# Last head group of the numerator in four matmuls of 108 rows, and the output projection held behind the numerator

## The chip, the cores and the metric

The kernel runs on one core of one Trainium2 chip. The metric is device time of one execution in microseconds (us), the median of three runs. The engines are PE (TensorE), DVE (VectorE), ACT (ScalarE), POOL (GpSimd) and SP (SyncE, which here only issues DMAs).

## The reference

A layer of linear attention with a learned feature map, beside a gated feed-forward network, for 2048 rows of width 576, 32 heads of 18 columns, and a hidden width of 4608 (fp32, cut to what matters):

```python
xn = layernorm(x)
qkv = xn @ wqkv                                   # 576 -> 3 x 576
pq, pk = q @ w_phi, k @ w_phi                     # per head, 18 x 18
phi_q = concat(softmax(pq), softmax(-pq))         # 36 features per head
phi_k = concat(softmax(pk), softmax(-pk))
kv = einsum("bhsf,bhsd->bhfd", phi_k, v)          # 36 x 18 per head
num = einsum("bhqf,bhfd->bhqd", phi_q, kv)        # the numerator
den = einsum("bhqf,bhf->bhq", phi_q, phi_k.sum(s)) + 1e-6
s = (num / den) @ wo                              # 576 x 576
ffn = (silu(xn @ w_gate) * (xn @ w_up)) @ w_down  # 576 -> 4608 -> 576
return x + s * silu(ffn)
```

## The kernel before

Most fp32 operands are split into a rounded fp32r part and a rest (`split`, L61: an ACT cast to `hi` and a DVE subtraction to `lo`), and a product is then three matmuls: hi by hi, hi by lo, lo by hi.

The program has these stages. Layer norm and the k and v side end in `kvp`, the sums of phi_k by v, one block for each head group and each sign of the softmax. A head group is seven heads, 126 columns; the fifth and last group has only four, 72 columns (`GROUPS`, `NL` = 72). The blocks are masked to the heads' own diagonal and split into `KVH` and `KVL` (L556 to L560).

The Q stage (loop over n near the end of the listing) goes over 2048 rows in eight passes of 256. `q_tile` computes phi_q times 1/den for 128 rows into the tile `e` (two signs by 576 columns): matmuls into the PSUM tile `p2`, of which there is one, then a chain on DVE and ACT (maximum, subtraction L316, exp, sums, `ez` L616, reciprocal, product L626). `numer` takes the two tiles of a pass and does for each head group four transposes (L638), a split of the 256 x 2 result into `ph` and `pl`, and six matmuls of 256 columns (L645: three products for each of two signs). The result goes, split again, into `oh` and `ol`; the last group's goes into `om` (named km), 108 rows deep: its hi part on 72 rows, and half of its lo part on 36 rows that two small DMAs from `lo` fill (L653). `project` multiplies by wo (L672, 14 matmuls of 288 columns for each of four half tiles), and ACT copies the result out (L678).

In the loop, `numer` of a pass comes first, then the two `q_tile`s of the next, then `project`. A list scheduler puts the instructions of each engine in order; the first four units of the feed-forward network's gate and up products (`early_tile`, matmuls into `pe`, L96) have low priority, and the scheduler puts their matmuls where PE would else wait. Those left over when the last `project` is issued run behind it. Their result goes to DRAM (`h_dram`, L136).

Then comes the main stage: for each further unit SP loads raw weights (`ld`, L738), POOL forms sums and differences of weight blocks (`ts`, L766 to L769), ACT and DVE split them into `w`, SP stores them (`w_dram`) and loads the small tails `wt`. The products px, py and pw (L790, L828) and the down product `pd` (L911) follow. The memory of `ld` is that of the Q stage, so the first load waits for the last wo matmul. This stage is not touched by the change.

## Time and profile before

| | before |
|---|---|
| median of 3 runs | 1592.99 us (1592.48 to 1593.02) |
| the profiled execution | 1592.74 us, of which the span is 1590.6 |
| PE busy | 1578.2 us, 99% of the span, 9383 matmuls |
| DVE, ACT, POOL busy | 1166.5, 724.8, 662.3 us |
| granted clock of TensorE | 0.999 of full speed, mean of the span |
| first matmul behind the last wo matmul | 457.65 us |
| first matmul of the main stage | 475.81 us |

Times in the trace count from the start of the span. Busy time on PE overlaps, since matmuls are pipelined: a row's duration is longer than the distance to the next row's start, and it is the distance that costs time.

### The profile page before, as it was taken

How to read it: one execution, taken by the hardware profiler on the slowest of the kernel's cores; microseconds unless marked ns; L12 is line 12 of the kernel's file. 1: busy time of each engine (PE TensorE's matmuls, PEld its weight loads, DVE VectorE, ACT ScalarE, POOL GpSimd, SP SyncE). 2: the span in 40 equal slices, each digit the busy share in tenths (PEclk: the TensorE clock that was granted, in tenths of full speed). 3: DMA queues.
4: the chain of work that ended last, by engine and by line, in shares of the span. 5: the costliest groups of instructions: out<-in, count | busy, mean ns of one | idle time of the engine just before them, and what ended most of it. 6: DMA issues, size and time to landing. Idle time of an engine off the chain costs nothing.

```text
span 1590.6 us, 25333 instructions
## 1 busy us (share of the span) xinstructions
PE 1578.2 (99%) x9383; PEld 1416.1 (89%) x9383; DVE 1166.5 (73%) x1729; ACT 724.8 (46%) x1403; POOL 662.3 (42%) x714
## 2 busy tenths in 40 slices
PE   9999999999999999999999999999999999999998
PEld 6899998999988988988888898888888888888887
DVE  7777769999946778887777778645767667666677
ACT  5633345455435654454544554454443343333334
POOL 3676762433116535554545445223324324133133
PEclk9999999999999999999999999999999999999999
DMA  9622244445447554555455453974545655555445
GB/s 306 200 82 81 95 145 129 119 122 163 165 175 245 174 178 174 176 177 180 174 174 200 163 186 116 337 219 151 154 139 156 192 177 160 176 184 184 142 118 179
DMA packets 124044, 269.03 MB, mean 169 GB/s; under 512 B 13194, under 2 KB 54858, under 8 KB 122642
## 3 DMA queue, kind: packets, MB, share of 16 engines
q1 hardware_dynamic: 108476, 245.49, 47.2%
q0 software_dynamic: 3552, 12.59, 2.7%
q10 hardware_dynamic: 11894, 9.35, 1.8%
q8 instruction: 74, 1.21, 0.3%
q14 instruction: 48, 0.39, 0.1%
HBM read 167.53 MB, written 99.09 MB: 168 GB/s over the span
## 4 chain that ended last, share of the span: by engine, by line
PE 67%; DVE 1%; POOL 1%; DMA 0%; issue 0%; ACT 0%; SPq 0%; POOLq 0%
PE px L790 25%; PE pd L911 24%; PE pw L790 12%; PE py L790 6%; DMA hb<-h_dram 0%; POOL acc L949 0%; PE pe L96 0%; DVE w L63 0%; DVE hh L63 0%; DMA out<-acc 0%; ACT w L62 0%; POOL ld L769 0%; DVE X L940 0%; POOL ha L1050 0%; DVE X L1073 0%
## 5 line engine op out<-in xcount | busy, mean ns | idle before, releaser
L911 PEld LDWEIGHTS pd<-dw,hh 128*128 128x128 f32 x3012 | 423.4, 188 | 22.4 <-ACT pd L966 1.5
L911 PE MATMUL pd<-dw,hh 128*128 128x288 f32 x3012 | 437.6, 295 | 1.9 <-ACT pd L966 0.7
L790 PE MATMUL px<-X,w 128*128 128x512 f32 x1512 | 385.7, 390 | 0.0
L790 PEld LDWEIGHTS px<-X,w 128*128 128x128 f32 x1512 | 274.6, 188 | 46.0
L790 PE MATMUL pw<-X,w 128*128 128x512 f32 x744 | 188.8, 389 | 0.0
L790 PEld LDWEIGHTS pw<-X,w 128*128 128x128 f32 x744 | 139.6, 188 | 28.9
L1073 DVE TENSOR_TENSOR acc<-pd,acc 128x576 f32<-128x576 f32 x128 | 96.2, 752 | 92.7 <-PE pd L911 92.1
L824 DVE TENSOR_TENSOR s<-pw,s 128x512 f32<-128x512 f32 x126 | 86.4, 687 | 90.3 <-ACT s L819 80.0
L819 ACT COPY s<-px 128x512 f32<-128x512 f32 x126 | 73.8, 586 | 145.4 <-PE px L790 145.3
L63 DVE TENSOR_TENSOR hh<-ha,hh 128x512 fp32r<-128x512 f32 x140 | 112.0, 826 | 19.6 <-ACT hh L62 19.3
L62 ACT CAST hh<-ha 128x512 fp32r<-128x512 f32 x140 | 82.7, 619 | 94.2 <-PE pd L911 68.7
L1045 POOL TENSOR_TENSOR hb<-hb 128x512 f32<-128x512 f32 x34 | 46.3, 1362 | 157.5 <-DVE hb L836 156.5
L96 PE MATMUL pe<-X,wh 128*128 128x512 f32 x340 | 106.0, 396 | 1.3 <-DVE h L135 0.6
L63 DVE TENSOR_TENSOR w<-ld,w 128x512 fp32r<-128x512 f32 (+1 forms) x96 | 77.2, 806 | 35.1 <-ACT w L62 34.1
L790 PE MATMUL px<-X,wt 128*128 128x512 f32 x252 | 98.0, 389 | 0.0
L790 PE MATMUL py<-X,w 128*128 128x512 f32 x378 | 96.5, 390 | 0.0
L1058 POOL TENSOR_TENSOR ha<-ha 128x512 f32<-128x512 f32 x34 | 52.6, 1563 | 102.1 <-DVE hh L63 102.1
L766 POOL TENSOR_TENSOR ts<-ld 128x256 f32<-128x256 f32 x32 | 26.8, 837 | 151.3 <-issue 72.6
L1032 POOL TENSOR_TENSOR h<-ha,hb 128x512 f32<-128x512 f32 x34 | 44.3, 1304 | 106.9 <-DVE ha L840 76.3
L62 ACT CAST w<-ld 128x512 fp32r<-128x512 f32 (+1 forms) x96 | 52.7, 550 | 74.9 <-POOL ld L769 42.3
L844 ACT COPY py<-px 128x512 f32<-128x512 f32 x63 | 36.1, 572 | 108.8 <-PE px L790 97.3
L790 PEld LDWEIGHTS py<-X,w 128*128 128x128 f32 x378 | 68.3, 188 | 10.8
(293 smaller groups left out, 3219.7 us busy)
## 6 DMA issues: line engine op xcount, KB each, us to landing
w_dram<-w SPq DMA_DIRECT2D x90, 512.0 KB
w<-w_dram SPq DMA_DIRECT2D x90, 512.0 KB
wt<-t_dram SPq DMA_DIRECT2D x62, 336.0 KB
ld<-in_B_w_gu SPq DMA_DIRECT2D x32, 512.0 KB
rt<-in_B_w_down SPq DMA_DIRECT2D x33, 288.0 KB
rb<-in_B_w_down SPq DMA_DIRECT2D x33, 288.0 KB
w_dram<-w SPq DMA_DIRECT2D x30, 256.0 KB
w<-w_dram SPq DMA_DIRECT2D x30, 256.0 KB
```

The source lines that it names most:

```text
L62: nc.scalar.copy(hi, src)
L63: nc.vector.tensor_sub(lo, src, hi)
L96: last = nc.tensor.matmul(ps, l, r, start=n == 0, stop=n == len(pairs) - 1)
L790: nc.tensor.matmul(ps, l, r, start=first and n == 0, stop=last and n == len(mm) - 1, skip_group_check=True)
L819: snaps.append(nc.scalar.copy(t, ps))
L824: nc.vector.tensor_add(t, ps, t)
L844: copies.append(nc.scalar.copy(yp, xp))
L911: nc.tensor.matmul(ps, l, r, start=first and n == 0 and m == 0, stop=n == len(hs) - 1 and m == 2, skip_group_check=True)
L1032: sub(s, g["h"][0][0], g["h"][0][1])
L1045: nc.gpsimd.tensor_add(a21, a21, g["h"][1][1])
L1058: sub(a12, a12, g["h"][0][0])
L1073: nc.vector.tensor_add(a2, pd[:, :, 0:HALF], a2)
```

## The change

The last head group's two signs are arranged so that 108 rows hold them. ACT makes a second copy of that part of `e` (`et`, two blocks of 108 columns for each sign's 72: the first 54 columns of both signs, then the last 18 columns of both signs three times over). Four transposes of `et` replace four of `e`. The first block gives 108 rows for three matmuls (hi by hi, hi by lo, lo by hi); the second block holds the last 18 columns three times, as hi, hi and lo, so that one matmul does all three products. `KVP`, which holds the matching rows of the masked blocks, is filled once by ten small DMAs from SBUF to SBUF on SP; what they read lies in an old buffer (`phi`). The split of the transposes is one ACT cast of 108 x 512 and two DVE subtractions (108 x 256, 36 x 256). The last group now comes second instead of first in a pass, and the wo matmuls of a pass, the last one excepted, are issued only after `done`, the last numerator matmul of that pass.

```diff
@@ KV blocks
+            km2 = kk.tile([P, 2 * D], F32R, name="phi", bufs=2)[0:NL, 0:4 * NL].rearrange("p (a s n) -> p a s n", a=2, s=2)
+            km2 = [km2[:, a] for a in range(2)]
...
-                split(KVH[0:w, 4 * i:4 * i + n, 0:w], KVL[0:w, 4 * i:4 * i + n, 0:w], km[0:w, 0:n, 0:w])
+                kh, kl = (t[0:w, 4 * i:4 * i + n, 0:w] for t in (KVH, KVL)) if n == 4 else km2
+                split(kh, kl, km[0:w, 0:n, 0:w])
+            KVP = qc.tile([NK, 3, NL], F32R, name="KVP")
+            for s in range(2):
+                for a, t in enumerate(km2):
+                    nc.sync.dma_start(KVP[s * N3:(s + 1) * N3, a].bitcast(F32), t[0:N3, s].bitcast(F32))
+                for b, t in enumerate((km2[0], *km2)):
+                    r = (2 * b + s) * DH
+                    nc.sync.dma_start(KVP[r:r + DH, 2].bitcast(F32), t[N3:NL, s].bitcast(F32))
@@ q_tile
-                return e
+                et = qk.tile([P, 2, NK], F32, name="et", bufs=2)
+                o = GROUPS[-1][0]
+                e2 = e.rearrange("p (s n) -> p s n", s=2)
+                nc.scalar.copy(et[:, 0].rearrange("p (s n) -> p s n", s=2), e2[:, :, o:o + N3])
+                nc.scalar.copy(et[:, 1].rearrange("p (b s n) -> p b s n", b=3, s=2),
+                               e2[:, :, o + N3:D].unsqueeze(1).to_broadcast([P, 3, 2, DH]))
+                return e, et
@@ numer
-                for g in (NG - 1, *range(NG - 1)):
+                for g in (0, NG - 1, *range(1, NG - 1)):
...
+                            src = e[0][:, s * D + o:s * D + o + w] if g < NG - 1 else e[1][:, s]
+                            nc.tensor.transpose(pt[0:w if g < NG - 1 else NK, s, j * P:(j + 1) * P], src, ident)
...
+                    else:
+                        nc.scalar.copy(ph[0:NK], pt[0:NK])
+                        nc.vector.tensor_sub(pl[0:NK, 0], pt[0:NK, 0], ph[0:NK, 0])
+                        nc.vector.tensor_sub(ph[0:2 * DH, 1], pt[0:2 * DH, 1], ph[0:2 * DH, 1])
+                        mm = [(KVP[:, a], p) for a, p in ((0, ph[0:NK, 0]), (1, ph[0:NK, 0]), (0, pl[0:NK, 0]), (2, ph[0:NK, 1]))]
+                    for k, (a, p) in enumerate(mm):
+                        done = nc.tensor.matmul(po[0:w], a, p, start=k == 0, stop=k == len(mm) - 1)
@@ project
-                        for k, (a, bw) in enumerate(mm):
-                            nc.tensor.matmul(ps[:, 0:HALF], a, bw, start=k == 0, stop=k == len(mm) - 1)
+                        with ExitStack() if last else tc.issue_after(done.ins):
+                            for k, (a, bw) in enumerate(mm):
+                                nc.tensor.matmul(ps[:, 0:HALF], a, bw, start=k == 0, stop=k == len(mm) - 1)
```

Line numbers of the changed kernel are higher: L96 becomes L97, L638 becomes L656, L645 becomes L669, L672 becomes L697, L766 to L769 become L791 to L794.

The scheduler's order changes with it. On PE, in the middle of the Q stage, the end of one pass's numerator stood before among the wo matmuls of the same pass (pt is the numerator, p the projection):

```order
L672 MATMUL p<-WOH,ol 128x288
L672 MATMUL p<-WOH,oh 128x288
L672 MATMUL p<-WOL,oh 128x288
L672 MATMUL p<-WOH,ol 128x288
L672 MATMUL p<-WOH,oh 128x288
L645 MATMUL pt<-ph,KVH 126x256 x2
L645 MATMUL pt<-ph,KVL 126x256 x2
L645 MATMUL pt<-pl,KVH 126x256 x2
L672 MATMUL p<-WOL,oh 128x288
L672 MATMUL p<-WOH,ol 128x288
```

In the changed kernel the same place has early matmuls (pe) ahead of the numerator's last six, and the wo matmuls all behind them:

```order
L97 MATMUL pe<-X_61,wh 128x512 x2
L97 MATMUL pe<-X_62,wh 128x512
L97 MATMUL pe<-X_62,wl 128x512
L97 MATMUL pe<-X_62,wh 128x512
L669 MATMUL pt<-ph,KVH 126x256 x2
L669 MATMUL pt<-ph,KVL 126x256 x2
L669 MATMUL pt<-pl,KVH 126x256 x2
L697 MATMUL p<-WOH,oh 128x288
L697 MATMUL p<-WOL,oh 128x288
```

So each pass now has its 56 wo matmuls in one piece, and early matmuls fill what they filled. Over the Q stage, from the first Q matmul to the last wo matmul, 324 early matmuls stand on PE instead of 290; behind the last wo matmul, ahead of the first py, 40 are left instead of 74.

On PE in the first pass, a run of early matmuls stands between the second and the third q tile. These are its last rows before and the first of the third tile (p with the input tile X_64):

```order
L96 MATMUL pe<-X_60,wl 128x512
L96 MATMUL pe<-X_60,wh 128x512 x2
L96 MATMUL pe<-X_61,wh 128x512
L96 MATMUL pe<-X_61,wl 128x512
L96 MATMUL pe<-X_61,wh 128x512 x2
L96 MATMUL pe<-X_61,wl 128x512
L96 MATMUL pe<-X_61,wh 128x512
L96 MATMUL p_2678<-QH,X_64 128x288
```

In the changed kernel the run ends seven matmuls earlier:

```order
L97 MATMUL pe<-X_60,wl 128x512
L97 MATMUL pe<-X_60,wh 128x512
L97 MATMUL p_2695<-QH,X_64 128x288
L97 MATMUL p_2695<-QL,X_64 128x288
L97 MATMUL p_2695<-QH,X_64 128x288 x2
```

It has 19 early matmuls instead of 26; the seven stand further behind, among the 324.

On POOL, at the opening of the main stage, the DMA that stores an early result stood before behind two units' sums:

```order
L603 DMA t_dram<-tl 32x896 x4
L766 TENSOR_TENSOR ts<-ld 128x256
L767 TENSOR_TENSOR ts<-ld,ts 128x256
L768 TENSOR_TENSOR ld<-ld 128x256
L769 TENSOR_TENSOR ld<-ld,ts 128x256
```

In the changed kernel one of these DMAs stands between the first and the second of them:

```order
L614 DMA t_dram<-tl 32x896 x4
L791 TENSOR_TENSOR ts<-ld 128x256
L137 DMA h_dram<-h 128x512
L792 TENSOR_TENSOR ts<-ld,ts 128x256
L793 TENSOR_TENSOR ld<-ld 128x256
L794 TENSOR_TENSOR ld<-ld,ts 128x256
```

The work of POOL, ACT and DVE on the first weights is otherwise in the order of before. The first px matmul writes a PSUM bank that the last early gate tile held; the ACT instruction that empties it (silu, L131) stands on ACT behind all casts of the first weight unit, the last of which waits for L794.

## Rows read from the trace of the kernel before

**Rows 1.** Windows: length; PE, PEld, DVE, ACT, POOL busy; clock; DMA.
```profile
320.00:340.00 20.00, 19.91 (x138) 18.64 (x137) 19.37 (x29) 9.57 (x15) 7.53 (x17) 1.00 0.43 132
...
440.00:460.00 20.00, 19.99 (x131) 17.46 (x130) 7.60 (x13) 7.75 (x16) 0.00 (x0) 1.00 0.13 41
```

**Rows 2.** Timeline of PE, a numerator's first groups: start, duration, line, tiles, count.
```profile
282.14 0.85 PE L638 MATMUL pt<-ident,e 128*72 128x128 f32 x6
282.74 0.48 PE L96 MATMUL pe<-X,wl 128*128 128x512 f32 x1
...
284.66 0.40 PE L645 MATMUL pt<-ph,KVH 72*72 72x256 f32 x2
...
285.37 0.40 PE L645 MATMUL pt<-ph,KVH 126*126 126x256 f32 x2
...
286.08 0.86 PE L96 MATMUL pe<-X,wh 128*128 128x512 f32 x3
```

**Rows 3.** Timeline of PE, eight transposes of 126 columns and what follows.
```profile
263.39 1.04 PE L638 MATMUL pt<-ident,e 128*126 128x128 f32 x8
264.19 0.38 PE L96 MATMUL p<-QL,X 128*128 128x288 f32 x1
```

**Rows 4.** Groups by line and form, weight loads of the transposes: busy, mean ns.
```profile
L638 PEld LDWEIGHTS pt<-ident,e 128*126 128x126 f32 x128 | 14.9, 140 | 1.1 <-issue 0.2 <-DVE lo L651 0.2
...
L638 PEld LDWEIGHTS pt<-ident,e 128*72 128x72 f32 x32 | 3.4, 114 | 1.7 <-DVE e L626 0.9 <-issue 0.3
```

**Rows 5.** Groups by line and form on DVE, 240 to 440 us.
```profile
L63 DVE TENSOR_TENSOR pl<-pt,ph 72x512 fp32r<-72x512 f32 x7 | 4.8, 683 | 0.1
...
L651 DVE TENSOR_TENSOR lo<-pt,km 72x256 fp32r<-72x256 f32 x7 | 2.9, 415 | 0.0
```

**Rows 6.** Timeline of PE, first matmul of the third q tile.
```profile
241.46 0.37 PE L96 MATMUL p<-QH,X 128*128 128x288 f32 x1
```

**Rows 7.** DVE timeline: last KV split, first ez, release of second tile's p2.
```profile
224.81 0.32 DVE L63 TENSOR_TENSOR KVL<-km,KVH 72x144 fp32r<-72x144 f32 x1 [0.38 <-ACT KVH L62]
...
235.80 1.35 DVE L616 TENSOR_TENSOR ez<-e,zb 128x1152 f32<-128x1152 f32 x1
...
240.55 0.76 DVE L316 TENSOR_TENSOR e<-p,m 128x576 f32<-128x576 f32 x1
```

**Rows 8.** Timeline of SP: two small SBUF to SBUF DMAs, first raw weight loads.
```profile
443.73 1.53 SPq L653 DMA_DIRECT2D km<-lo  x2
...
457.89 1.30 SPq L738 DMA_DIRECT2D ld<-in_B_w_gu  x2
```

**Rows 9.** PE timeline: last early matmuls, first of the main stage.
```profile
457.65 0.39 PE L96 MATMUL pe<-X,wh 128*128 128x512 f32 x1
...
464.45 1.21 PE L96 MATMUL pe<-X,wh 128*128 128x512 f32 x3
...
472.46 0.50 PE L96 MATMUL pe<-X,wh 128*128 128x512 f32 x1 [0.63 <-DVE h L135]
...
475.81 0.39 PE L828 MATMUL py<-X,w 128*128 128x512 f32 x1
```

**Rows 10.** Timeline of POOL: the first weight unit's sums.
```profile
463.17 0.73 POOL L766 TENSOR_TENSOR ts<-ld 128x256 f32<-128x256 f32 x1 [50.78 <-DMA ld<-in_B_w_gu]
463.98 1.07 POOL L767 TENSOR_TENSOR ts<-ld,ts 128x256 f32<-128x256 f32 x1
...
465.70 0.74 POOL L769 TENSOR_TENSOR ld<-ld,ts 128x256 f32<-128x256 f32 x1
...
472.86 0.57 POOL L136 DMA_DIRECT2D h_dram<-h  x1 [1.95 <-DVE h L135]
```

**Rows 11.** Timeline of ACT: last cast of the first weight unit, the last silu.
```profile
467.31 0.40 ACT L62 CAST w<-ld 128x256 fp32r<-128x256 f32 x1
...
471.86 0.60 ACT L131 ACTIVATE h<-pe 128x512 f32<-128x512 f32 x1 [0.52 <-PE pe L96]
```

**Rows 12.** Timeline of DVE: an early product at the opening of the main stage.
```profile
464.37 0.68 DVE L135 TENSOR_TENSOR h<-pe,h 128x512 f32<-128x512 f32 x1
```

More of the change, by code (lines that the diff above doesn't have):

```diff
@@ L31 @@
 NK = NL + NL // 2
+N3 = NK // 2
 QS = 256
@@ L531, in gated_hedgehog_kernel @@
             qc = att.enter_context(tc.tile_pool(name="qc", bufs=1, reuse_waits="tile"))
-            KVH = qc.tile([GW, 2 * NG, GW], F32R, name="KVH")
-            KVL = qc.tile([GW, 2 * NG, GW], F32R, name="KVL")
+            KVH = qc.tile([GW, 2 * NG - 2, GW], F32R, name="KVH")
+            KVL = qc.tile([GW, 2 * NG - 2, GW], F32R, name="KVL")
             zb = qc.tile([P, 2 * D], F32, name="zb")
@@ L637, in numer @@
                         for j, e in enumerate(es):
-                            nc.tensor.transpose(pt[0:w, s, j * P:(j + 1) * P], e[:, s * D + o:s * D + o + w], ident)
+                            src = e[0][:, s * D + o:s * D + o + w] if g < NG - 1 else e[1][:, s]
+                            nc.tensor.transpose(pt[0:w if g < NG - 1 else NK, s, j * P:(j + 1) * P], src, ident)
                     ph = qk.tile([GW, 2, QS], F32R, name="ph", bufs=2)
                     pl = qk.tile([GW, 2, QS], F32R, name="pl", bufs=2)
-                    split(ph[0:w], pl[0:w], pt[0:w])
                     po = pt[:, 0]
-                    for k, (a, p) in enumerate(((KVH, ph), (KVL, ph), (KVH, pl))):
-                        for s in range(2):
-                            nc.tensor.matmul(po[0:w], a[0:w, 2 * g + s, 0:w], p[0:w, s], start=k + s == 0, stop=k + s == 3)
+                    if g < NG - 1:
+                        split(ph[0:w], pl[0:w], pt[0:w])
+                        mm = [(a[0:w, 2 * g + s, 0:w], p[0:w, s]) for a, p in ((KVH, ph), (KVL, ph), (KVH, pl)) for s in range(2)]
+                    else:
[5 more added lines that the diff above has]
+                        done = nc.tensor.matmul(po[0:w], a, p, start=k == 0, stop=k == len(mm) - 1)
                     if g < NG - 1:
@@ L653, in numer, with project @@
                         nc.sync.dma_start(om[NL:NK, a].bitcast(F32), lo[a * (NK - NL):a * (NK - NL) + NK - NL].bitcast(F32))
-                return oh, ol, om
-            def project(b, oh, ol, om, last):
+                return oh, ol, om, done
+            def project(b, oh, ol, om, done, last):
                 for j in range(QS // P):
```

## The prediction

> **What bounds the kernel now.** I read the windows first, to see which engine the Q stage waits for. PE is busy for 19.91 of 20 us in the middle of it, while DVE is close behind with 19.37, and ACT has half its time free [rows 1]. Both PE and DVE are nearly full because the scheduler fills PE's waits with early matmuls. That is work that has to be done anyway. So the time of the stage is PE's work, plus what PE waits where no filler stands. After 440 us DVE is busy for 7.60 of 20 us only [rows 1]: its part of the stage is over while PE still has the wo matmuls of the last pass. The granted clock is full in both windows. Then I read PE's timeline by distances from start to start. A change to this stage counts in three places: the number of matmuls, the places where PE meets a wait without a filler, and the early matmuls that are left at the end, which cover the loading of the first weights of the main stage.
>
> **The matmuls removed.** Each of eight passes has four matmuls for the last group instead of six. Six matmuls of 256 columns with 72 rows take from 284.66 to 285.37, and six with 126 rows from there to 286.08, 0.71 us each time [rows 2]. So one costs 0.118 us whatever its rows, and 108 rows, which lie between, cost that too. 16 x 0.118 = **-1.9 us**. This is firm, since PE's work is what sets the time.
>
> **The transposes.** There are as many as before, with 108 columns instead of 72. Six of them, three of 72 and three of 126 columns by the order, take 0.60 us [rows 2]; eight of 126 take 0.80 us [rows 3]. Both are 0.10 us each: the wider ones cost **nothing** more. The weight load by itself does grow, from 114 to 140 ns for 54 more columns [rows 4]. The Trainium skill (TensorE: Matmul & The Clock Gate, section LDWEIGHTS) says that a load's time is its columns divided by 1.2, in ns, with rows not counting, which is 30 ns for 36 more columns, and by it, if loads set the pace, the 32 transposes would cost 0.96 us more; the trace agrees in direction (26 ns for 54 columns, where the rule has 45). The distances in rows 2 and 3 show the pace unmoved, so the sum takes 0. The upper end, from the measured loads alone, is 36/54 of 26 ns, 17 ns, 32 times: 0.6 us.
>
> **The subtractions and copies.** On DVE one subtraction of 512 columns, 0.683 us, becomes two of 256 columns at 0.415 us each [rows 5]: 0.15 us more in a pass, 1.2 us in the stage. On ACT there are 32 copies more, of 108 columns in two halves; the nearest row is a cast of 256 columns at 0.40 us [rows 11], so they take up to 0.4 us each, at most 13 us of an engine that is half free [rows 1]. I cost both at nothing. The cover is that PE gets later than DVE: 34 more early matmuls (7.7 us at 0.227 us each, below) stand ahead of the last wo matmul, so what DVE delivers has that much more time. Without the cover, DVE's 1.2 us would come in full.
>
> **The wo matmuls behind the numerator.** They cost the same, only later. What is new is that early matmuls alone stand between a group's transposes and its numerator matmuls. Behind the last numerator matmul come nine wo matmuls (0.132 us each) that need only groups 0 to 2, so the last group's `oh` and `ol` have 1.2 us for an ACT cast and a DVE subtraction of 0.415 us [rows 5]. That is enough if DVE isn't just in one of its long operations, as the 1.35 us of `ez` [rows 7]. I take 0; ends -2 (fewer short waits, as PE is later) and +1.5 us (one such operation in one pass in seven).
>
> **A new wait in the first pass.** There is one `p2`. The third q tile starts on PE at 241.46 [rows 6], just as DVE's subtraction of the second tile frees it: 240.55 + 0.76 = 241.31 [rows 7], and 0.15 us to get there. In front of it, seven early matmuls are gone to a later place. Early matmuls have a distance of 0.227 us: from 457.65 to 464.45 are 30 of them in 6.80 us [rows 9]. PE would be there 1.59 us earlier, at 239.87, and DVE has the same chain of work ahead of its subtraction. So PE waits **+1.6 us**, and the seven matmuls still have to be done. The ends are 0 (DVE gets there sooner) and 2.8, with the next paragraph.
>
> **The ten DMAs for KVP.** They are issued on SP behind the last KV split, which ends at 225.13 [rows 7]. One SBUF to SBUF DMA took 0.77 us to issue [rows 8], so ten are out by 232.8. `ez` of the first q tile and the first `et` copies use memory that these DMAs read, and wait until they have landed. `ez` started at 235.80 [rows 7], 3.0 us later. The landing isn't in these rows; the nearest, a 512 KB load, took from 457.89 [rows 8] to 463.17, when POOL could use it [rows 10], 5.3 us with its wait for the queue. By that, `ez` would be up to 2.3 us late, and with small DMAs rather under 3.0. I take 0, because KVP's pieces are a few KB. Of a delay, what comes behind `ez` on DVE, the subtraction that frees `p2` among it, would be late by as much. I count at most 1.2 of it as the upper end above.
>
> **The opening of the main stage.** Behind the last wo matmul 74 early matmuls took from 457.65 to 475.81, 18.16 us [rows 9]. At 0.227 they need 16.8. The other 1.36 us are waits: around 464.45, where three matmuls show 1.21 us, and at 472.46, where the profile names the DVE product `h` [rows 9]. DVE and ACT are late there because they split the first weights in between. With the 34 matmuls done earlier, the early products that met this work are fewer, and I take both waits away: **-1.4 us** (ends -1.4 and 0).
>
> What comes in their place: 40 matmuls are over 9.1 us after the last wo matmul, and py takes 0.2 more, so PE wants px at +9.3 us. The raw weights come no earlier, since their load waits for the last wo matmul. Before, POOL began at 463.17, which is +5.5, and its fourth operation ended at 465.70 + 0.74, +8.8 [rows 10]. The `h_dram` DMA that now stands between the first and the second costs 0.57 [rows 10], so +9.4. The last cast (0.40) and the silu (0.60) follow on ACT [rows 11], to +10.4. PE is free at +9.3: **+1.1 us**. The lower end is 0.5 (the DMA's issue delays POOL by nothing); the upper 2.2, if the DMA has first to wait for its DVE product, which in before ended at 464.37 + 0.68 = 465.05 [rows 12], 1.1 us behind POOL's first operation.
>
> **Sum.** -1.9 + 0 + 1.6 - 1.4 + 1.1 = -0.6 us. The profiled execution took 1592.74 us (its span 1590.6 and 2.1 around it), 0.25 under the median of 1592.99, so the sum gives 1592.1 from the one and 1592.4 from the other; I say **1592.3 us**. A measurement of this kernel can tell about 0.2%, 3.2 us, from no change.
>
> **Rivals.**
>
> *No wait comes, faster.* If DVE frees `p2` earlier and the silu is ready in time, the two new waits go: -1.9 - 1.4 = -3.3; with the lower end of the passes -5.3. So 1587.5 to 1589.5 us. For it: PE is the bound and the change removes work from it. Against: both waits follow from the order on one engine and rows on another. Chance 0.17.
>
> *The opening has too little cover, slower.* Before, PE had 18.2 us of early matmuls while the first weights were loaded, summed, split and stored, and it has 9.1 now. DMA traffic of the first units is the same, and its start is tied to the last wo matmul, so px, the second unit and pd come 9 us sooner against it. If the second unit's weights, the tails `wt` or the `hb` loads for pd end later than PE's need, PE waits for what is missing: 3 to 6 us, up to the 9.1 that was lost. It decides where a transfer that before landed less than 9 us ahead of its use isn't sped up by the earlier start. -0.6 + 3 to 6: 1594.7 to 1598.2 us, with 1596 the middle. For it: all of the weights are loaded behind the same matmul. Against: the first px needs only unit 1, which I have counted. Chance 0.20.
>
> *Stalls in the passes.* DVE is 97% busy [rows 1] and the fillers are used up in a fixed order; a late `ol` in each of seven passes by half a long operation, 0.5 us, costs 3.5: 1595.8 us. Against: PE is up to 7.7 us later than it was. Chance 0.10.
>
> *Weight loads set the pace of the transposes*: +0.6 by the measured loads, 1592.9 us, no change that can be told. The rule above says so, and rows 2 and 3 speak against it. Chance 0.05.
>
> My forecast has 0.48. **Chances**: faster by over 0.2% (under 1589.8) 0.17; slower by over 0.2% (over 1596.2) from half of the second rival and a third of the third, 0.13; within 0.2%, 0.70. The **range** is 1588.5 to 1596.5 us: below it some half of the first rival (0.09), above it the upper part of the second and a little of the third (0.11).
>
> **What would show it.** In the profile after: 224 numerator matmuls in the Q stage at 0.118; the third q tile's first matmul behind a wait of about 1.6 us on DVE L317 at 240 to 241.5; transposes at 0.10; no gap over 0.3 us among the 40 early matmuls behind the last wo matmul; the first px about 10.4 us behind it, with a wait of about 1 us on the silu. It is wrong if PE waits in the middle of the passes, if a DMA of the main stage's first units ends a wait of PE, or if `ez` waits on the KVP DMAs.

## The result and the profile after

The changed kernel took 1597.05 us (median of 7 runs, 1594.12 to 1598.68), the kernel before 1592.99. The ratio is 1.0025, interval 1.0015 to 1.0035: about 4 us slower, beyond the range of the prediction and on the other side of no change. The seven runs lie in two groups, 1594.1 to 1594.7 us with a granted clock of 0.998 to 1.000 over the span and 1597.1 to 1598.7 us with 0.997 to 0.998, and the profiled execution (1597.25 us, span 1595.4, clock 0.998) is of the upper one.

The page's first part has PE less busy than before, 1575.6 instead of 1578.2 us, with the 16 matmuls fewer:

```profile
PE 1575.6 (99%) x9367; PEld 1415.4 (89%) x9367; DVE 1166.3 (73%) x1737; ACT 732.6 (46%) x1437; POOL 663.1 (42%) x714
```

The waits of PE over the whole execution (line, what was waited for, sum, times, longest) show where it stood instead. The waits for `et`, for the q tile's PSUM (`e` L317) and those of px are new; the waits for `xn` were 0.8 us before and lie in the first 50 us, and the first Q matmul comes 0.2 us earlier than before all the same (221.21, 221.42):

```profile
PE px L815 <- ACT s L844: 3.0, 2, 2.5
PE tp L219 <- DVE xn L207: 2.4, 2, 1.7
PE pt L656 <- ACT et L641: 2.1, 1, 2.1
PE p L97 <- DVE e L317: 1.7, 1, 1.7
...
PE px L815 <- ACT py L869: 0.9, 1, 0.9
...
```

PE's timeline of the first pass has the two waits there. The third q tile starts at 241.52, as before [rows 6], but PE had been free since 239.8. The first transpose of `et` is late by 2.1 us, and the early matmuls behind it with it:

```profile
239.40 0.39 PE L97 MATMUL pe<-X,wh 128*128 128x512 f32 x1
241.52 0.37 PE L97 MATMUL p<-QH,X 128*128 128x288 f32 x1 [1.73 <-DVE e L317]
...
247.73 0.32 PE L656 MATMUL pt<-ident,et 128*108 128x128 f32 x1 [2.13 <-ACT et L641]
```

What the `et` copy waited for stands ahead of it on ACT, a cast of an early unit's raw weights, and that waited for a DMA:

```profile
246.66 0.83 ACT L67 CAST wh<-raw 128x768 fp32r<-128x768 f32 x1 [2.26 <-DMA raw<-in_B_w_gu]
247.40 0.28 ACT L641 COPY et<-e 128x108 f32<-128x108 f32 x1
```

DVE waited 1.74 us for the same cast. And the DMA was late on SP's queue. The ten KVP DMAs took it from 224.69 to 232.35, and the raw loads, behind everything that they pushed back, began at 239.99:

```profile
224.69 1.72 SPq L568 DMA_DIRECT2D KVP<-phi  x2
...
230.17 2.18 SPq L571 DMA_DIRECT2D KVP<-phi  x3
...
239.99 9.38 SPq L114 DMA_DIRECT2D raw<-in_B_w_gu  x3
```

In the kernel before they began at 234.68:

```profile
234.68 11.63 SPq L113 DMA_DIRECT2D raw<-in_B_w_gu  x3
```

Inside a pass all is as the prediction had it. Four matmuls of 108 rows take from 288.50 to 288.97, 0.118 us each as in [rows 2], and six transposes, three of 126 and three of 108 columns, from 285.74 to 286.37, 0.105 each:

```profile
285.74 0.55 PE L656 MATMUL pt<-ident,e 128*126 128x128 f32 x3
286.12 0.49 PE L656 MATMUL pt<-ident,et 128*108 128x128 f32 x3
286.37 0.38 PE L97 MATMUL p<-QL,X 128*128 128x288 f32 x1
...
288.50 0.40 PE L669 MATMUL pt<-ph,KVP 108*72 108x256 f32 x2
288.73 0.28 PE L669 MATMUL pt<-pl,KVP 108*72 108x256 f32 x1
288.85 0.28 PE L669 MATMUL pt<-ph,KVP 108*72 108x256 f32 x1
288.97 0.40 PE L97 MATMUL pe<-X,wh 128*128 128x512 f32 x1
```

The end of the Q stage and the opening of the main stage answer to [rows 9]. The last wo matmul starts at 465.23 instead of 457.52, 7.7 us later. The 40 early matmuls run without a wait, and py is reached at 474.45, 1.4 us earlier than before. From there on px waits four times, the last time 2.53 us, and the `pd` matmuls behind that wait take 3.08 us for twelve where they take 1.75 a little ahead of it:

```profile
465.23 0.30 PE L697 MATMUL p<-WOL,km 108*128 108x288 f32 x1
...
474.45 0.39 PE L853 MATMUL py<-X,w 128*128 128x512 f32 x1
475.06 1.66 PE L815 MATMUL px<-X,w 128*128 128x512 f32 x6 [0.22 <-ACT h L132]
...
479.52 1.65 PE L815 MATMUL px<-X,w 128*128 128x512 f32 x6 [0.89 <-ACT py L869]
...
483.47 1.66 PE L815 MATMUL px<-X,w 128*128 128x512 f32 x6 [0.48 <-ACT s L844]
...
507.44 1.75 PE L936 MATMUL pd<-dw,hh 128*128 128x288 f32 x12
511.71 1.70 PE L815 MATMUL px<-X,w 128*128 128x512 f32 x6 [2.53 <-ACT s L844]
...
513.64 3.08 PE L936 MATMUL pd<-dw,hh 128*128 128x288 f32 x12
```

The first raw weights of the main stage, whose memory the last wo matmul frees, are loaded at 465.61, where it was 457.89 before [rows 8]. This is SP's queue:

```profile
465.61 1.30 SPq L763 DMA_DIRECT2D ld<-in_B_w_gu  x2
```

The longest of the waits of px is followed back over two engines. On POOL's timeline the fourth weight unit's sums came late, from 504.28 on, and ended at 508.66:

```profile
504.28 1.18 POOL L791 TENSOR_TENSOR ts<-ld 128x256 f32<-128x256 f32 x1
...
507.48 1.18 POOL L794 TENSOR_TENSOR ld<-ld,ts 128x256 f32<-128x256 f32 x1
```

In the kernel before the last of these four sums ended at 499.75, 8.9 us earlier:

```profile
499.02 0.73 POOL L769 TENSOR_TENSOR ld<-ld,ts 128x256 f32<-128x256 f32 x1
```

On ACT's timeline the last cast of that unit waited 3.73 us for them, and the copy `s` that px needs stands behind it:

```profile
508.70 0.41 ACT L63 CAST w<-ld 128x256 fp32r<-128x256 f32 x1 [3.73 <-POOL ld L794]
...
511.08 0.58 ACT L844 COPY s<-px 128x512 f32<-128x512 f32 x1
```

Windows of 4 us around it show the granted clock in the third column from the end: full until 512 and 0.65 on average in the next window, so that most of it was at the lower level, 1.2 GHz. PE had been busy for 1.47 of 4 us in the window ahead of the fall:

```profile
508.00:512.00 4.00, 1.47 (x10) 1.24 (x10) 1.98 (x4) 3.30 (x7) 1.57 (x3) 1.00 0.62 206
512.00:516.00 4.00, 4.00 (x17) 3.63 (x17) 3.31 (x5) 1.97 (x5) 2.03 (x2) 0.65 0.92 324
```

**Where the 5 us went.** The last matmul of the program starts at 1584.07 before and at 1589.17 after, 5.1 us later. From the starts of all PE matmuls, with what is over their usual distances counted as waits: the first Q matmul earlier, -0.2; 16 matmuls fewer, -1.9; the two waits of the first pass, about +3.9; shorter waits in the passes behind it, -1.8; the waits among the last early matmuls that were there before, -1.4; and from the first py to the start of the last matmul 1114.7 us instead of 1108.3, +6.5. The sum is +5.1. Some 1.5 us of the +6.5 are matmuls at the lower clock.

### The profile page after: what moved, and what is told of

The parts are those of the page before. It is cut to its first block, busy times and chain, and to the rows that moved or that the text cites. A ratio compares the mean times of both kernels' runs of the same rounds, so it can differ in the third digit from the quotient of the medians.

```text
span 1595.4 us, 25391 instructions
## 1 busy us (share of the span) xinstructions
PE 1575.6 (99%) x9367; PEld 1415.4 (89%) x9367; DVE 1166.3 (73%) x1737; ACT 732.6 (46%) x1437; POOL 663.1 (42%) x714
## 4 chain that ended last, share of the span: by engine, by line
PE 93%; DMA 2%; DVE 2%; POOL 1%; issue 1%; ACT 1%; SPq 1%; POOLq 0%; ACTq 0%; DVEq 0%
PE px L815 25%; PE pd L936 24%; PE pw L815 12%; PE p L97 7%; PE py L815 6%; PE pe L97 4%; PE p L697 4%; PE kvp L333 2%; PE pt L669 2%; PE vx L421 1%; PE pt L656 1%; PE vw L421 1%; PE tp L252 1%; DMA h_dram<-h 1%; PE vx L97 1%
## 5 line engine op out<-in xcount | busy, mean ns | idle before, releaser
L97 PE MATMUL pe<-X,wh 128*128 128x512 f32 x340 | 107.1, 397 | 0.0
L791 POOL TENSOR_TENSOR ts<-ld 128x256 f32<-128x256 f32 x32 | 27.8, 867 | 152.1 <-issue 69.7
```

The costliest lines, as they stand in the source:

```text
L97: last = nc.tensor.matmul(ps, l, r, start=n == 0, stop=n == len(pairs) - 1)
```

## The experiments

Each kernel was measured five times or more, beside the kernel before; "ratio to before" is the 95% interval. "Last wo" is the start of the last wo matmul, "early behind" the early matmuls that are left behind it, and "end" the start of the program's last matmul, all of the one profiled execution, from PE's timeline; where the executions of a kernel differ, that one need not be the median.

| kernel | median us | ratio to before | last wo | early behind | first py | end | end - last wo |
|---|---|---|---|---|---|---|---|
| before | 1592.99 | | 457.52 | 74 | 475.81 | 1584.07 | 1126.5 |
| after | 1597.05 | 1.0015 to 1.0035 | 465.23 | 40 | 474.45 | 1589.17 | 1123.9 |
| e1_four_only | 1601.64 | 1.0047 to 1.0071 | 470.65 | 40 | 479.87 | 1594.48 | 1123.8 |
| e2_hold_only | 1592.21 | 0.9993 to 1.0010 | 462.72 | 48 | 473.74 | 1586.75 | 1124.0 |
| e3_kvp_pool | 1597.60 | 1.0024 to 1.0048 | 465.27 | 40 | 474.49 | 1587.69 | 1122.4 |
| e3b_kvp_act | 1599.94 | 1.0035 to 1.0061 | 467.68 | 40 | 476.89 | 1591.86 | 1124.2 |
| f2_no_kvp_dma | 1592.75 | 0.9996 to 1.0014 | 461.98 | 40 | 471.20 | 1584.18 | 1122.2 |
| e7_keep1 | 1599.76 | 1.0037 to 1.0062 | 465.90 | 78 | 484.07 | 1592.20 | 1126.3 |
| d1_dve_more | 1602.84 | 1.0051 to 1.0079 | 466.92 | 31 | 474.08 | 1594.31 | 1127.4 |
| d2_pe_back | 1600.19 | 1.0040 to 1.0065 | 470.01 | 41 | 479.46 | 1591.93 | 1121.9 |
| t1_tails_pool | 1603.69 | 1.0058 to 1.0083 | 472.23 | 47 | 483.04 | 1594.50 | 1122.3 |
| f10_bare_six | 1592.49 | 0.9994 to 1.0011 | 457.75 | 75 | 475.96 | 1584.09 | 1126.3 |
| f7_bare_nohold | 1595.90 | 1.0016 to 1.0038 | 463.74 | 41 | 473.18 | 1586.57 | 1122.8 |
| f5_bare | 1597.47 | 1.0021 to 1.0046 | 466.52 | 41 | 475.97 | 1588.93 | 1122.4 |
| h1_bare_cap | 1595.30 | 1.0009 to 1.0027 | 458.89 | 73 | 477.01 | 1585.81 | 1126.9 |
| h2_after_cap | 1606.06 | 1.0073 to 1.0099 | 469.25 | 73 | 487.28 | 1595.64 | 1126.4 |
| g2_hold_cap | 1598.42 | 1.0021 to 1.0046 | 461.45 | 75 | 479.38 | 1587.36 | 1125.9 |

### The two halves of the change, KVP's queue, and the cover given back

**e1_four_only:** the changed kernel without the hold.

```diff
-                        with ExitStack() if last else tc.issue_after(done.ins):
+                        with ExitStack():
```

> The changed kernel without the hold on the wo matmuls; the four matmuls, et, KVP and the group order stay. By the order 40 early matmuls are still left behind the last wo matmul, 19 stand in the run ahead of the third q tile, and POOL's order at the opening of the main stage is the changed kernel's. Theory A (the loss is two waits in the first pass, 1.7 and 2.1 us, and an opening of the main stage that has lost its cover, about 6 us): the time stays at that of the changed kernel, 1594 to 1598.5 us, with a wait of about 1.7 us of the third q tile, about 2.1 us of the first et transpose, and 4 to 6 us of waits from 475 to 520 us. Rival B (holding the wo matmuls back costs the time): back to about 1591 to 1592 us.

It is 4.6 us slower still, so the hold isn't what costs; beside these four matmuls it helps. The last wo matmul is 5.4 us later than with the hold, and the wait for `et` comes three times, 4.4 us in sum. Rival B fell; A had the direction of the opening's waits, but not these.

**e2_hold_only:** the kernel before with `done` and the hold.

```diff
...
-                        for k, (a, bw) in enumerate(mm):
-                            nc.tensor.matmul(ps[:, 0:HALF], a, bw, start=k == 0, stop=k == len(mm) - 1)
+                        with ExitStack() if last else tc.issue_after(done.ins):
+                            for k, (a, bw) in enumerate(mm):
+                                nc.tensor.matmul(ps[:, 0:HALF], a, bw, start=k == 0, stop=k == len(mm) - 1)
```

> The kernel before with the hold on the wo matmuls alone. By the order 48 early matmuls are left behind the last wo matmul instead of 74, the run ahead of the third q tile has 26 as before, and there are no KVP DMAs. Theory A: no wait in the first pass; the opening has 5.9 us less cover and POOL's order there changes as well, so some 2 to 5 us of its waits come: 1593 to 1597 us. Rival B (holding the wo matmuls back costs the time by waits inside the passes): about 1596 to 1597 us, with PE waits between 270 and 460 us that are over 2 us in sum. Rival C (the four matmuls and what they bring are alone to blame): 1592 to 1593 us.

No change in time. Its parts are there all the same: from the first Q matmul to the last wo matmul, PE's excess over the usual distances falls from 6.4 to 4.4 us, and 26 more early matmuls go ahead of that last wo matmul, which is 5.2 us later. The profiled execution took 1595.23 us, 3 us over the median; it had waits of 2.5 us in the opening, and the granted clock was 0.61 from 504 to 508 us. So in this execution the hold gains about 2 us in the passes and gives back more; that the others lose less in the opening is likely by the median, but wasn't traced.

**e3_kvp_pool** and, after it, **e3b_kvp_act:** the KVP DMAs on another queue, POOL's and then ACT's (`nc.scalar`). One of the two lines changed:

```diff
-                    nc.sync.dma_start(KVP[s * N3:(s + 1) * N3, a].bitcast(F32), t[0:N3, s].bitcast(F32))
+                    nc.gpsimd.dma_start(KVP[s * N3:(s + 1) * N3, a].bitcast(F32), t[0:N3, s].bitcast(F32))
```

> The changed kernel with the ten KVP DMAs issued on POOL's queue instead of SP's; the order of all else is unchanged. Theory A (on SP the ten DMAs, 7.7 us of issue, push the raw loads of the early units back by 5.3 us; the wh cast that waits for them stands on ACT ahead of the first et copies, and PE waits 2.1 us): the raw loads are issued at about 234.7 again, the et wait is gone, and the time is about 2 us below the changed kernel's, 1594 to 1596 us; the third q tile still waits 1.7 us. Rival D (the et copies are late by the split of wo or by the memory that KVP's sources hold): the wait of about 2 us stays and the time with it.

> The changed kernel with the ten KVP DMAs issued on ACT's queue, where ACT is idle for 7 us at that place; on POOL they had pushed POOL's sums, and by these SP's raw loads, as far back as on SP. Theory A and C: the raw loads are issued at 235 us or earlier instead of 240, DVE's wait of 1.7 us for their cast and PE's of 2.1 us for et go, the last wo matmul is 1.5 to 3 us earlier than 465.2, and the time as much below the changed kernel's: 1594 to 1596 us. Rival D (the first pass is not what makes the end): the last wo matmul stays at 465 and the time at 1597.

Neither helped, but neither did what was meant. On POOL the ten issues took 5.1 us from the sums that stood behind them, SP's stores of these sums came later, and the raw loads were issued at 239.37, hardly earlier than in the changed kernel. The `et` wait went, and the wait for the third q tile grew from 1.7 to 3.7 us. On ACT the ten held the first pass back by 2.4 us more. That DMAs can be put on an idle queue for nothing was wrong on both.

**e7_keep1:** the changed kernel with the last early tile behind the last numerator matmul.

```diff
+                for j in (1,) if f == 1 else (0, 1):
+                    with tc.issue_after(om[3].ins) if (f, i, j) == (EARLY - 1, 0, 1) else ExitStack():
+                        early_tile(f, i, parts, (j,), behind=read[2 * NT + 1] if f == 1 else None)
```

> The changed kernel with the last early tile (28 matmuls) held behind the last pass's last numerator matmul. By the order 78 early matmuls are left behind the last wo matmul instead of 40, and POOL's order there is that of the kernel before. Nothing is changed in the first pass. Theory A: the waits of 6 us between 475 and 520 us go, and 1.4 us of waits among the early matmuls come back: about 5 us below the changed kernel, 1591.5 to 1593.5 us. Rival E (the early matmuls are missed in the passes, where PE now waits for DVE): waits of 4 us or more between 360 and 465 us and no gain, 1595 to 1599 us.

Both were right, in one half each. With 78 early matmuls behind the last wo matmul every wait of the opening is gone: 1108.1 us from py to the end, as in the kernel before (1108.3). But the last wo matmul came no earlier (465.90), though 38 early matmuls, 8.6 us, were taken from ahead of it, and DVE's last product of `e` ended at 446.24, where it ends at 446.80 with them. These are the waits of PE from 225 to 520 us that came in their place:

```profile
PE pt L656 <- DVE e L637: 2.9, 1, 2.9
PE pt L669 <- DVE pl L64: 2.1, 3, 0.8
PE p L97 <- DVE e L317: 1.7, 1, 1.7
...
PE pt L656 <- DVE ol L64: 1.3, 1, 1.3
```

So at that place early matmuls had been put where PE would else wait for DVE. The waits cost more than their length here: behind the one of 2.9 us the granted clock was 0.50 from 448 to 452 us, so that this run makes the loss of holding back look larger than its waits alone.

### PE's work against DVE's

**d1_dve_more** and **d2_pe_back** add work to one engine.

```diff
                     split(ph[0:w], pl[0:w], pt[0:w])
+                    if g == 0:
+                        nc.vector.tensor_sub(pl[0:w], pt[0:w], ph[0:w])
```

> The kernel before with one DVE subtraction of 512 columns (0.68 us) done a second time in each of eight passes, 5.5 us of DVE work that changes no result. By the order the scheduler moves 43 early matmuls into the Q stage, 31 are left behind the last wo matmul. Theory C (the Q stage ends when DVE's chain lets it, PE is only filled; the raw weights of the main stage start with the last wo matmul, and from it to the end the rest can't be done in less than about 1123 us, where the kernel before has 1126.5): the last wo matmul is 5 to 9 us later than 457.5 and the end 2.5 to 7 us later, 1595 to 1599 us. Rival P (PE's work bounds, DVE's is hidden, as predicted): 1592 to 1593 us.

> The changed kernel with two of the four matmuls of the last group done a second time in each pass, so that there are six again (the numerator of the last group is then not the reference's: its lo parts count twice). 16 matmuls, 1.9 us of PE's work, come back. Theory C: the last wo matmul stays within 1 us of 465.2, PE is 1.9 us later at the first py and waits 1.9 us less behind it, and the time is the changed kernel's within 1 us. Rival P: 1.9 us more than the changed kernel, about 1598 to 1600 us.

5.5 us more on DVE cost the kernel before 10.2 us (1592.68 beside it): the last wo matmul is 9.4 later. So DVE's work isn't free. That DVE's chain holds PE up is not shown by it, though: from 225 us to the last wo matmul PE waits 0.2 us in all, and the 43 early matmuls, 9.8 us, that the scheduler put ahead of that matmul are enough to make it late. Behind it px waits 8.0 us, 5.3 of them for `s`, and the granted clock was 0.50 from 516 to 520 us. d2 decides less than it was meant to: its scheduler order differs, with a wait of 2.4 us for `pl` in the fifth pass and a granted clock of 0.57 from 372 to 376 us behind it; the last wo matmul is 4.8 us later and the time 3 us longer, more than either theory gave.

**t1_tails_pool:** an SBUF to SBUF subtraction moved from DVE to POOL in the changed kernel.

```diff
-                nc.vector.tensor_sub(t, t, hi)
+                nc.gpsimd.tensor_sub(t, t, hi)
```

> The changed kernel with the subtraction of the small weight tails (128 x 896, eight of 1.08 us in the Q stage) on POOL instead of DVE: 8.7 us off DVE's chain, PE's work unchanged. By the order 47 early matmuls are left behind the last wo matmul instead of 40. Theory C: the last wo matmul is 3 to 8 us earlier than 465.2 and the time 3 to 5 us below the changed kernel's, 1591 to 1594 us. Rival P: no change, 1597 us. Rival F (POOL then is late with its own work): waits on POOL in the opening and no gain.

The time rose by 6.6 us instead. DVE's busy time from 225 us to the last product of `e` stayed at 202.8 us, as in the changed kernel (202.5): what was taken off it came back in another form, told at the end. So this run doesn't test the theory.

### Only taking work away

**f10_bare_six** and **f7_bare_nohold** differ in nothing but the 16 matmuls; **f5_bare** is the second with the hold. In these, as in f2 and h1 below, KVP is filled with other blocks than the reference asks for; the instructions have the same shapes. Their common edit to the changed kernel:

```diff
-                return e, et
+                return e, e.rearrange("p (s n) -> p s n", s=2)[:, :, D - NK:D]
...
-                        nc.vector.tensor_sub(pl[0:NK, 0], pt[0:NK, 0], ph[0:NK, 0])
-                        nc.vector.tensor_sub(ph[0:2 * DH, 1], pt[0:2 * DH, 1], ph[0:2 * DH, 1])
+                        nc.vector.tensor_sub(pl[0:NK], pt[0:NK], ph[0:NK])
...
+            nc.scalar.copy(KVP[:, 0:2], KVH[0:NK, 0:2, 0:NL])
+            nc.scalar.copy(KVP[:, 2], KVL[0:NK, 0, 0:NL])
```

> A bare form of the changed kernel that keeps six matmuls for the last group: no et copies (the transposes read 108 columns of e itself), one DVE subtraction of 108 x 512 instead of two, KVP filled by two ACT copies instead of ten DMAs (its numbers and so the last heads' numerator are not the reference's), no hold, and the two lo matmuls done twice. What is left of the change is the transposes of 108 columns, 108 rows in the matmuls, and the group order. By the order 75 early matmuls are left behind the last wo matmul, as before. Theory G (the removal of matmuls itself makes the scheduler put more early matmuls into the passes) and the first pass theory alike: as before, 1591.5 to 1593.5 us, the last wo matmul at 456 to 459 us. Rule of the wider weight loads: up to 1 us more.

> The same bare form with the two repeated matmuls taken out: 16 matmuls fewer, nothing else. By the order 41 early matmuls are left behind the last wo matmul. Theory G: the last wo matmul is 4 to 9 us later than in the form with six and the time 2 to 7 us longer, 1594 to 1600 us, though work was only taken away. Rival H (what costs is the first pass: KVP's DMAs, et and the raw loads behind them): 1.9 us faster than the form with six, 1590 to 1591.5 us, the last wo matmul at 460 or earlier.

> The bare form with four matmuls and the hold on the wo matmuls. By the order 41 early matmuls are left behind the last wo matmul, 26 stand ahead of the third q tile. Theory G: the hold takes 2 us of short waits off PE and keeps the numerator from waiting behind wo matmuls; the last wo matmul at 461 to 464 us and the time 1592 to 1596 us, below the form without the hold. Rival H: 1589 to 1591 us.

The form with six is the kernel before in time, in the last wo matmul and in the early matmuls behind it. With four it is 3.4 us slower: the last wo matmul is 6.0 us later, which is 34 early matmuls more ahead of it (7.7 us) less the 1.9 us taken out; py is 2.8 us earlier; and the waits of PE from 225 to 520 us are nearly all in the opening:

```profile
PE px L804 <- ACT s L833: 2.4, 2, 2.0
PE px L804 <- ACT h L132: 1.1, 1, 1.1
PE px L804 <- ACT py L858: 0.5, 1, 0.5
...
```

That is theory G, without any of the new copies and DMAs; the clock is full in both profiled executions up to the last few us. The hold made the bare form no faster (1.6 us slower in the medians, with intervals that overlap); it has a wait of 1.9 us for `pl` in the fifth pass and a granted clock of 0.63 from 368 to 372 us behind it. Why the hold helps one order and not the other stays open.

**f2_no_kvp_dma:** the changed kernel, hold, `et` and all, with only the ten DMAs replaced by the two copies above.

> The changed kernel with its et copies, two subtractions and hold, but KVP filled by two ACT copies instead of ten DMAs (the last heads' numerator is not the reference's). By the order 26 early matmuls stand ahead of the third q tile and 40 are left behind the last wo matmul. Rival H: the raw loads are issued at about 235 us again, the waits of 1.7 and 2.1 us in the first pass go, the last wo matmul is 3 us earlier than 465.2 and the time 2.5 to 4 us below the changed kernel's, 1593 to 1595 us. Theory G: the first pass is only a part, the time at most 2 us below the changed kernel's, 1595 to 1598 us.

The first pass is a larger part than theory G gave it: 4.3 us below the changed kernel, level with before. The raw loads are issued at 235.26, the waits of 1.7 and 2.1 us are gone, and the last wo matmul is 3.3 us earlier. It still has the 40 early matmuls and waits of 3.9 us on px; with py at 471.20, 4.6 us earlier than before, they return what was gained. So waits in the opening alone don't make a kernel slower than before. Nor is SP's queue all that the DMAs change: without them the scheduler leaves 26 early matmuls ahead of the third q tile, as before, and this run doesn't part the one from the other.

### Holding early matmuls back

**h1_bare_cap**, **h2_after_cap** and **g2_hold_cap** put back the number of early matmuls ahead of the last wo matmul that the kernel before has. The edit of the second and third, which hold six tiles, not five (the first holds one only, (2, 0, 1) behind pass 4):

```diff
+                    dones.append(om[3].ins)
...
+                    n = {(2, 0, 0): 2, (2, 0, 1): 3, (3, 1, 0): 4, (3, 1, 1): 6, (3, 0, 0): 6, (3, 0, 1): 7}.get((f, i, j))
+                    with tc.issue_after(dones[n - 1]) if n else ExitStack():
+                        early_tile(f, i, parts, (j,), behind=read[2 * NT + 1] if f == 1 else None)
```

> The bare form with four matmuls and no hold on wo (its last heads' numerator is not the reference's), with one early tile held back until pass 4's last numerator matmul, so that by the order 291 early matmuls stand in the Q stage instead of 323, spread nearly as in the kernel before, and 73 are left behind the last wo matmul. Theory G (the early matmuls put ahead of the last wo matmul are what costs): the last wo matmul at 456 to 459 us instead of 463.7, no waits over 0.7 us behind it, and 1590 to 1591.5 us: the 1.9 us that the removed matmuls are worth appear. Rival E (PE needs these early matmuls against DVE's chain): PE waits 3 us or more for DVE between 300 and 460 us, the last wo matmul at 461 or later, 1593 to 1597 us.

> The changed kernel with five of the early tiles held back until the last numerator matmul of passes 2, 3, 4, 6 and 7, so that by the order 291 early matmuls stand in the Q stage instead of 324, 73 behind it. The first pass is the changed kernel's. Theory G: the last wo matmul at 458 to 461 us, no waits over 0.7 us behind it, 1592 to 1594 us: the two waits of the first pass (3.8 us) are left and eat the 1.9 us of the matmuls and the 2 us of the hold. Rival E: PE waits for DVE in the passes instead, the last wo matmul at 463 or later, 1595 to 1600 us.

> The kernel before with the hold on the wo matmuls and with the same early tiles held back, 289 early matmuls in the Q stage and 75 behind it, as in the kernel before. Theory G: the 2 us of short waits that the hold took off PE show in the end, the last wo matmul at 455.5 to 458 us, 1590 to 1591.5 us, faster than both kernels. Rival E: PE waits for DVE in the passes, 1592.5 to 1596 us.

In all three px's waits in the opening are gone, as G had it, and the gain is not there, as E had it. Where the early matmuls were held back PE waits for DVE; in h2, from 225 to 520 us:

```profile
PE p L97 <- DVE e L317: 4.3, 2, 2.5
PE pt L669 <- DVE pl L64: 3.3, 3, 1.5
PE pt L656 <- DVE ol L64: 1.5, 1, 1.5
PE pt L656 <- ACT et L641: 1.1, 1, 1.1
...
```

In h2 and g2 the clock fell behind such waits too, to 0.73 from 408 to 412 us and 0.67 from 392 to 396. The bare form, whose clock stayed full there, comes nearest and is the clean test: its last wo matmul is at 458.89, but that is still 1.1 us behind the form with six matmuls, not 1.9 ahead of it, and PE waits 2.6 us in its passes, 1.4 of it for `pl`. No version beat the kernel before.

## Why the prediction was wrong

**What set the time.** The last column of the table shows it. From the last wo matmul to the end the six kernels with 73 or more early matmuls left behind it take 1125.9 to 1126.9 us, and the eight with 40 or 41 take 1121.9 to 1124.2: of the 7.7 us that 34 matmuls are worth, 2 to 5 come back. That wo matmul itself moves over almost 15 us, and within each of the two groups the time follows it. It is when the main stage's first raw weights can be loaded: 457.89 before [rows 8], 465.61 after. Then come POOL's sums, the casts, the stores and the next units. The early matmuls lie beside that chain: 18 us of them before, 9 us after. With 18 the chain is covered and PE's work counts; with 9 PE reaches px sooner than the weights do, and waits.

**The step that failed** is "The opening of the main stage", with its term of +1.1 us: it measured +6.5 (1114.7 us from the first py on instead of 1108.3). I counted the first px only. The silu before it, on which I put 1.1, cost 0.4; then px waited three more times, 3.9 us, as the units behind came late, and about 1.5 us went in the stretch at the lower clock behind the longest wait, which the prediction has no term for. The rival "the opening has too little cover, slower" said 1594.7 to 1598.2 us, and that is what came; it had a chance of 0.20 against 0.48. (Its lower end takes the -0.6 off twice: 1592.74 - 0.6 + 3 is 1595.1.)

**Behind it stands the sentence that 34 early matmuls ahead of the last wo matmul are cover.** I read them as time given to DVE, which makes DVE's 1.2 us free, and not as 7.7 us by which the weight loads start later. f10 and f7 show it alone: 16 matmuls taken out, 1.9 us of work, and the last wo matmul 6.0 us later. e7 and the three caps show why the early matmuls couldn't simply be left for the end: PE then waits for DVE. The last wo matmul follows 18 to 19 us behind DVE's last product of `e`. These are the products' rows before, after, in f10, in f7 and in h1:

```profile
438.07 1.36 DVE L626 TENSOR_TENSOR e<-e,y 128x1152 f32<-128x1152 f32 x1
...
445.44 1.36 DVE L637 TENSOR_TENSOR e<-e,y 128x1152 f32<-128x1152 f32 x1
...
438.18 1.36 DVE L633 TENSOR_TENSOR e<-e,y 128x1152 f32<-128x1152 f32 x1
...
443.56 1.36 DVE L633 TENSOR_TENSOR e<-e,y 128x1152 f32<-128x1152 f32 x1
...
439.52 1.36 DVE L633 TENSOR_TENSOR e<-e,y 128x1152 f32<-128x1152 f32 x1
```

DVE has the same work in f10, f7 and h1, and h1 is f7 with one tile held back. So of the 5.4 us by which f7's product is later than f10's, 4.0 come with the early matmuls that PE does first; from 225 us to that product DVE is idle for 13.0 us in f10, 17.4 in f7 and 14.9 in h1. In none of these orders could the stage use PE's saving: it went into early matmuls, or, with them held back, into waits. DVE at 19.37 of 20 us [rows 1] fits that; that no order could use it isn't shown. "PE's work is what sets the time", on which the -1.9 rests, held only while the opening was covered.

**The ten DMAs for KVP**, costed at nothing, were the second miss. `ez` was not late by them (235.59, 235.80 before), which is all I looked at. The queue behind them was: the loads of wo came 3.9 and the raw loads 5.3 us later, and a cast that waited for these stood on ACT ahead of `et`. Without the DMAs the kernel is 4.3 us faster (f2), where the wait for `p2` went as well; of the 5.0 us by which the last matmul starts earlier in the two profiled executions, 3.3 are there at the last wo matmul, and the rest lies behind it, where only the changed kernel's clock fell.

**What was right.** The price of a matmul (0.118 us) and of a transpose (0.10 to 0.105 us, whatever its columns); f10, whose transposes are the wider ones, is within 0.9994 to 1.0011 of before. By the Trainium skill (TensorE: Matmul & The Clock Gate, section LDWEIGHTS), where a load's time goes with its columns, an estimate is 0.96 us more if loads set the pace; the distances show none of it, though f10's interval alone is too wide to tell. The wait for `p2`, +1.6, measured 1.73. The waits among the last early matmuls, -1.4, went. Short waits inside the passes fell by 1.8 us, within the bounds of -2 to +1.5 where I took 0.

**What stays open.** Why the scheduler puts 34 early matmuls more into the passes when 16 others are taken out. An order by itself moves the time by as much as the change does: f2 and f5 have the same DMAs, hold and matmuls and nearly the same early matmuls behind the last wo, differ in the `et` copies and one subtraction, and lie 4.7 us apart (1592.75, 1597.47). So it isn't settled how much of the 4 us is this one order, and how much four matmuls would cost in any. How much of it is the clock stays open too: an execution of the changed kernel with a mean clock of 1.000 wasn't traced.

## What to carry to other kernels

Filler work that is moved ahead is not free: ask what starts only when the work behind it is done (here a memory that the next stage's loads wait for), and count the moved time on that start. Where two engines are both nearly full, look at the other before taking work off one: here the saving found no place in any order tried. And ask of a small DMA what stands behind it in its queue, not only when it lands: here loads came 5.3 us later behind ten of them.

## What the runs showed of the hardware

A subtraction on POOL and `ez` on DVE, both from SBUF to SBUF, held each other up. In t1 the six `ez` that started well inside one of POOL's took 2.07 to 3.27 us instead of 1.35: about their own time and what was left of POOL's. This is one of POOL's subtractions on its timeline, one of 2.1 us as most are:

```profile
279.69 2.10 POOL L611 TENSOR_TENSOR tl<-tl,th 128x896 f32<-128x896 f32 x1 [7.35 <-ACT th L610]
```

And this is DVE's timeline, one `ez` at the same time and one with POOL idle when it starts:

```profile
279.74 3.27 DVE L627 TENSOR_TENSOR ez<-e,zb 128x1152 f32<-128x1152 f32 x1
297.27 1.35 DVE L627 TENSOR_TENSOR ez<-e,zb 128x1152 f32<-128x1152 f32 x1
```

At 352.75 us it was POOL's that took longer, 3.48 us, and the `ez` beside it took 1.34. In sum the sixteen `ez` took 29.7 us instead of 21.6: of the 8.7 us taken off DVE 8.1 came back as longer instructions of DVE.

And a wait of PE can cost more than its length. Behind the 2.53 us of the changed kernel the granted clock fell, and twelve `pd` matmuls took 3.08 us. In f2 the same px waited 2.25 us, the clock stayed full, and the same twelve took 1.75:

```profile
508.31 1.66 PE L811 MATMUL px<-X,w 128*128 128x512 f32 x6 [2.25 <-ACT s L840]
...
510.03 1.75 PE L932 MATMUL pd<-dw,hh 128*128 128x288 f32 x12
```
